# Gated delta attention and squared-ReLU MoE layer on one core: the start of the kernel put in another order, and three weight parts prepared ahead where there were two

## The chip, the cores and the metric

The kernel runs on one core of a Trainium2 chip. The metric is the device time of one execution in microseconds. Besides TensorE (PE, with its weight loads PEld), VectorE (DVE), ScalarE (ACT) and GpSimd (POOL) the core has SyncE (SP), which in this kernel issues every DMA.

## What is computed

For each of 4 batches and 8 heads a 48 by 48 state is carried over 768 tokens: the key is divided by its norm plus 1e-6, the output of a token is its query times the state so far, and then the state takes up beta times the outer product of the key and (value minus what the state holds for that key). The outputs of all heads, 3072 tokens of 384 numbers, go through a layer `relu(x @ w_in)` squared `@ w_out` with 2048 hidden columns. The two weight matrices arrive as 64-bit floats; all else is float32.

## The kernel before

The attention is done in 12 units (`u`), each 128 tokens of two batches with all 8 heads, in two chunks of 64 tokens per head. A unit goes through these stages:

- `load`, `load_q`, `load_beta`, `load_v` (L199 to L230): keys, queries, betas and values, by DMAs of 96 KB (betas 2 KB). A key tile is `kpad`; the second unit's queries use the third `kpad` tile.
- `normalize` (L232): ScalarE squares the keys (L241), VectorE sums them (L242), ScalarE takes the root (L244), VectorE inverts it with one Newton step (L245 to L251) and scales the keys (L253).
- `static` (L263): TensorE transposes keys and queries (L284), ScalarE copies them out (L285), TensorE multiplies keys with keys and keys with queries (L294). For the first two units ScalarE copies the products out (L327, L337) and GpSimd masks the second kind (L340). The triangular blocks go to DRAM and come back in another layout as `lt` (L311, L319).
- `invert` (L353): 31 pairs of VectorE instructions (L380 or L382, and L383), each needing the one before, invert triangular blocks. For the first two units one such chain handles both (`invert(ds_[0])`). The inverse goes to DRAM as `inv` (L389) and comes back as `tt` (L398) and `t1t` (L403); GpSimd clears the second unit's `tt` (L394) once that memory has been read.
- `whole` and `sequential` (L406, L455; together `state_part`, seven pieces): the inverse is completed (L421 to L433), applied (L441, L448), and the state is carried on (L471 to L495).

`moe` (L500) takes a finished unit through the two weight matrices with 3-term products in reduced precision (L540, L527). That needs the weights as a high and a low part. `split_weights` (L135) makes them in 28 parts of 512 or 384 columns, in this order per part: ScalarE takes an absolute value (`least`, L142), GpSimd a maximum (L143), VectorE four bit operations (`words`, L150 to L157), ScalarE copies the high part (L160), TensorE forms the low part with three products (`low`, L166) and ScalarE copies it (L167). A generator does one part per `take`; `low` of a part stands behind `words` of the next. `far` (L173) says how many parts have their `least` written ahead, and `room` (L131) gives the parts scratch tiles alternately from two pools, with two buffers for each name. `fetch(n)` (L122) issues the loads of the next n parts.

Inside `tc.manual_schedule` the order of instructions on PE, SP, DVE and ACT is the order in which the program text emits them. POOL's order is not set by hand. Every engine and SP's queue run their instructions strictly in that order, so an instruction that waits holds back all that stand behind it.

Until L675 the program is written out by hand: loads, the first two units' `normalize` and `static`, the first inverse, the third unit's `normalize` and the first unit's `state_part`, with 19 takes of the split between. This is called the start below. Then a loop (L676) over units 1 to 11 weaves the parts of a unit by fractions of its length (`weave`, L578): the rest of the split (in unit 1 only), the next unit's `static` and `invert`, this unit's `state_part`, loads and `normalize` of the unit after next (`loads`, L599), and the previous unit's `moe`.

Of the kernel before, what the change touches and what calls it, by code (L numbers as in the profile page):

```python
# [20 lines left out]
def kernel(  # L21
# [92 lines left out]
    NW = len(weight_parts)  # L114
# [5 lines left out]
    AHEAD = 20  # L120

    def fetch(n):  # L122
        for _ in range(n):
            x = len(raws)
            if x < NW:
                src = weight_parts[x][2]
                raw = wpool.tile([P, src.shape[1], 2], I32, name=place[x])
                nc.sync.dma_start(out=raw.rearrange("p a b -> p (a b)"), in_=src.bitcast(I32))
                raws.append(raw)
# [5 lines left out]
    def split_weights():  # L135


        def least(x):

            w1 = raws[x][:, :, 1]  # L140
            a, rest = room(x, w1.shape[1])
            nc.scalar.activation(out=a.bitcast(F32), in_=w1.bitcast(F32), func=AF.Abs)  # L142
            nc.gpsimd.tensor_scalar(out=a.bitcast(F32), in0=a.bitcast(F32), scalar1=LEAST, scalar2=None, op0=ALU.max)  # L143
            return x, a, rest

        def words(x, a, rest):
            raw = raws[x]
            w1 = raw[:, :, 1]

            nc.vector.tensor_scalar(out=a, in0=a, scalar1=3, scalar2=0x3FFFFFF8,  # L150
                                    op0=ALU.logical_shift_left, op1=ALU.bitwise_and)

            nc.vector.scalar_tensor_tensor(out=a, in0=w1, scalar=-0x40000000, in1=a,  # L153
                                           op0=ALU.bitwise_and, op1=ALU.bitwise_or)

            nc.vector.tensor_scalar(out=w1, in0=a, scalar1=-0x800000, scalar2=None, op0=ALU.bitwise_and)
            nc.vector.scalar_tensor_tensor(out=rest.bitcast(F32R), in0=raw[:, :, 0].bitcast(U32), scalar=2.0 ** -52,  # L157
                                           in1=w1.bitcast(F32), op0=ALU.mult, op1=ALU.mult)
            hl = wpool.tile([P, 2, raw.shape[1]], F32R, name=place[x])
            nc.scalar.copy(out=hl[:, 0], in_=a.bitcast(F32))  # L160
            return x, a, rest, hl

        def low(x, a, rest, hl, bank):
            ps = bank()[:, :hl.shape[2]]
            for n, (m, y) in enumerate(((ident, a.bitcast(F32)), (minus, hl[:, 0]), (plus, rest.bitcast(F32R)))):
                nc.tensor.matmul(ps, lhsT=m, rhs=y, start=(n == 0), stop=(n == 2))  # L166
            nc.scalar.copy(out=hl[:, 1], in_=ps)  # L167
            halves[weight_parts[x][:2]] = hl[:, 0], hl[:, 1]

        before, ready = None, []  # L170
        for x in range(NW):

            far = 2 if x < AHEAD - 2 else 1  # L173
            while x + len(ready) < min(NW, x + far):
                ready.append(least(x + len(ready)))
            if x == 0:
                yield
            now = words(*ready.pop(0))
            if before:
                low(*before, split_bank)  # L180
            before = now
            if x + 1 + len(ready) < min(NW, x + 1 + far):
                ready.append(least(x + 1 + len(ready)))
            yield
        low(*before, split_bank)
        yield
# [17 lines left out]
    def load(u):  # L204
        t0, b0 = (u // NU) * P, (u % NU) * 2
        d = dict(u=u, t0=t0, b0=b0, y=[None] * NC, marks={})
        d["kp"] = kpad[u % 3]
        load_to(d["kp"], k, d, D)
        return d
# [22 lines left out]
    def normalize(d):  # L232

        n2, s0, s1 = [apool.tile([P, H2], F32, name=f"{n}{d['u'] % 2}", bufs=1) for n in ("n2", "s0", "s1")]
        kn = d["kp"].rearrange("p c h d -> p (c h) d")[:, :, :D]
        for c in range(NC):
            h = slice(c * H, (c + 1) * H)

            sq = (apool.tile([P, H, D], F32, name="r", bufs=2) if d["u"] == 2 else
                  spool.tile([P, PC], F32, name="rest")[:, :H * D].rearrange("p (h e) -> p h e", h=H))  # L240
            nc.scalar.activation(out=sq, in_=kn[:, h], func=AF.Square)  # L241
            nc.vector.tensor_reduce(out=n2[:, h], in_=sq, axis=AX.X, op=ALU.add)  # L242
            yield
        nc.scalar.activation(out=s0, in_=n2, func=AF.Sqrt)  # L244
        nc.vector.tensor_scalar(out=s1, in0=s0, scalar1=1e-30, scalar2=None, op0=ALU.max)  # L245
        nc.vector.reciprocal(out=s1, in_=s1)
        yield
        nc.vector.tensor_tensor(out=s1, in0=s1, in1=n2, op=ALU.mult)
        nc.vector.tensor_tensor(out=s1, in0=s1, in1=s0, op=ALU.add)
        nc.vector.tensor_scalar(out=s1, in0=s1, scalar1=0.5, scalar2=1e-6, op0=ALU.mult, op1=ALU.add)  # L250
        nc.vector.reciprocal(out=s1, in_=s1)  # L251
        yield
        nc.vector.tensor_tensor(out=kn, in0=kn, in1=s1.unsqueeze(2).broadcast_to(list(kn.shape)), op=ALU.mult)  # L253
        yield
# [365 lines left out]
    L1, N1 = (0.22, 0.42), (0.62, 0.92)  # L620
# [7 lines left out]
    engines = {mybir.EngineType.PE, mybir.EngineType.SP, mybir.EngineType.DVE, mybir.EngineType.Activation}  # L628
    with tc.manual_schedule(engines=engines):
        ds_ += [load(0), load(1)]  # L630
        fetch(F0)
        load_beta(ds_[0])
        load_q(ds_[0])
        load_q(ds_[1])
        load_beta(ds_[1])
        fetch(F1)
        take(normalize(ds_[0]))
        take(splits, 1)
        take(normalize(ds_[1]))
        pair = [static(d) for d in ds_[:2]]  # L640
        for d in pair:
            take(d, 2)
# [8 lines left out]
        for d in pair:  # L651
# [5 lines left out]
            take(d, 1)  # L657
            take(splits, 1)
        ds_.append(load(2))
        load_v(ds_[1])  # L660
        load_q(ds_[2])
        load_beta(ds_[2])
        fetch(NW)
        take(invert(ds_[0]))
        third = normalize(ds_[2])
        take(third, 2)
        for _ in range(3):
            take(splits, 1)
            take(third, 1)
# [6 lines left out]
        for u in range(1, units):  # L676
            parts = [(splits, NS, 0, 0.88, "")] if u == 1 else []
            if inverse:
                parts.append((inverse, NI - n_i, 0, I1 - 1, "quiet"))
            getting = loads(u)  # L680
            parts += [(getting, 2, *L1, "quiet"), (getting, 5, *N1, "quiet")]
            if u < units - 1:
                parts.append((static(ds_[u + 1]), 2, *A1))
            parts.append((state_part(ds_[u]), 7, *Q1))
            if before:
                parts += [(before, OVER + 1, 0, E2, ""), (before, 1, 0.2, 0.24, "quiet")]
            before = moe(ds_[u - 1])
            inverse = invert(ds_[u + 1]) if u < units - 1 else None
            if inverse:
                parts.append((inverse, n_i, I0, 1, "quiet"))  # L690
            parts.append((before, n_moe - OVER, M0, M1, ""))
            weave(*parts)
# [32 lines left out]
```

## Time and profile before

| | |
|---|---|
| median of 3 runs | 710.51 us (708.12 to 711.27) |
| the profiled execution | 708.47 us, its span from first to last instruction 706.8 us |
| busy in the span | PE 637.2 us (90%), DVE 427.0 (60%), ACT 332.2 (47%), POOL 73.3 (10%) |
| granted TensorE clock | 0.969 of 2.4 GHz in the mean |

All times of the trace are microseconds from the first instruction. Parts of the weights are numbered from 0 in the order of the split: 0 to 2, 7 to 9 and so on have 512 columns, the others 384. A busy time is the sum over an engine's instructions; an engine that is not busy waits for a semaphore or has its instructions issued late. Busy time on PE is not PE at its peak.

### The profile page before, as it was taken

The page shows a single profiled execution, that of the slowest core. Times are in us where ns is not written, and L with a number is a line of the kernel's source. Part 1 is how long each engine was busy: PE and PEld are TensorE (multiplying, and loading weights), DVE is VectorE, ACT ScalarE, POOL GpSimd, SP SyncE. Part 2 cuts the span into 40 slices and gives each one's busy share as a digit, 9 for nine tenths or more (in the row PEclk, how much of TensorE's full clock was granted, in tenths as well). Part 3 has the DMA queues.
Part 4 walks back from the last instruction along what each step waited for, and adds up shares of the span by engine and source line. Part 5 has one row for each costly group of instructions (what it writes and reads, how often), then busy time and mean ns, then how long its engine had stood idle before and what let it go on. Part 6 is the DMA issues. An engine that isn't in the chain of part 4 may idle for free.

```text
span 706.8 us, 23318 instructions
## 1 busy us (share of the span) xinstructions
PE 637.2 (90%) x10104; PEld 589.9 (83%) x10104; DVE 427.0 (60%) x1165; ACT 332.2 (47%) x632; POOL 73.3 (10%) x86
## 2 busy tenths in 40 slices
PE   1820698798999999999999999999999999999997
PEld 1600267697999999999999999999999999999996
DVE  4789775568468467577576494684675764641111
ACT  3730466454553554544545535535445445355252
POOL 6440342210100100001001001001000010000000
PEclk9965799999999999999999999999999999999999
DMA  7888501400450531522603504406315124030100
GB/s 171 183 221 327 129 3 27 88 2 2 71 105 2 112 65 18 118 43 37 137 5 53 122 3 77 99 4 120 55 21 121 36 38 93 3 61 3 25 1 22
DMA packets 172134, 49.92 MB, mean 71 GB/s; under 512 B 163840, under 2 KB 166912, under 8 KB 172032
## 3 DMA queue, kind: packets, MB, share of 16 engines
q1 hardware_dynamic: 172032, 48.44, 31.7%
q8 instruction: 79, 1.29, 0.8%
q14 instruction: 23, 0.19, 0.1%
HBM read 37.32 MB, written 11.01 MB: 68 GB/s over the span
## 4 chain that ended last, share of the span: by engine, by line
PE 80%; issue 4%; DMA 4%; SPq 3%; DVE 3%; POOL 2%; ACT 2%; POOLq 0%; DVEq 0%
PE h L540 29%; PE o L527 29%; PE g L471 3%; PE g L448 3%; PE g L492 3%; SPq L202 2%; DMA w<-in_moe_w_in_dram 2%; PE x L294 2%; PE x L441 2%; PE x L484 2%; PE x L284 1%; POOL a L143 1%; PE g L284 1%; PE g L294 1%; DMA inv<-tt 1%
## 5 line engine op out<-in xcount | busy, mean ns | idle before, releaser
L527 PE MATMUL o<-w,h_h 128*128 128x384 f32 x768 | 204.2, 347 | 0.0
L540 PE MATMUL h<-x_h,w 128*128 128x256 f32 x1152 | 172.3, 285 | 2.1 <-ACT x_h L509 1.2
L519 DVE TENSOR_TENSOR h_l<-r,h_h 128x512 fp32r<-128x512 f32 x96 | 66.1, 688 | 153.4 <-PE o L527 60.7
L540 PEld LDWEIGHTS h<-x_h,w 128*128 128x128 f32 x1152 | 152.5, 188 | 6.1 <-ACT x_h L509 2.6
L547 ACT ACTIVATE r<-h 128x512 f32<-128x512 f32 x96 | 57.4, 598 | 175.0 <-PE h L540 172.3
L527 PEld LDWEIGHTS o<-w,h_h 128*128 128x128 f32 x768 | 133.9, 189 | 2.5
L527 PE MATMUL o<-w,h_l 128*128 128x384 f32 x384 | 130.2, 339 | 0.0
L382 DVE SCALAR_TENSOR_TENSOR tmp<-lt,bt,z 128x126 f32<-128x126 f32 (+22 forms) x310 | 96.1, 310 | 15.1 <-DMA lt<-blocks 6.7
L540 PE MATMUL h<-x_l,w 128*128 128x256 f32 x576 | 99.0, 280 | 0.0
L383 DVE TENSOR_TENSOR z<-z,tmp 128x126 f32<-128x126 f32 (+22 forms) x310 | 79.2, 255 | 10.6
L540 PEld LDWEIGHTS h<-x_l,w 128*128 128x128 f32 x576 | 81.4, 188 | 0.0
L527 PEld LDWEIGHTS o<-w,h_l 128*128 128x128 f32 x384 | 72.4, 189 | 0.0
L548 ACT ACTIVATE r<-r 128x512 f32<-128x512 f32 x96 | 60.7, 632 | 3.1
L550 ACT CAST h_h<-r 128x512 fp32r<-128x512 f32 x96 | 59.5, 620 | 3.1
L366 POOL MEMSET z<- 128x512 f32 x10 | 5.2, 525 | 397.6 <-DMA inv<-z 397.6
L166 PE MATMUL o<-r,plus 128*128 128x512 f32 (+1 forms) x16 | 9.8, 699 | 30.8 <-DVE r L153 30.8
L242 DVE TENSOR_REDUCE n<-rest 128x8 f32<-128x384 f32 x22 | 12.0, 550 | 38.5 <-ACT rest L241 38.5
L143 POOL TENSOR_SCALAR a<-a 128x384 f32<-128x384 f32 (+1 forms) x18 | 24.2, 1345 | 63.4 <-ACT a L142 48.3
L166 PEld LDWEIGHTS o<-r,plus 128*128 128x128 f32 x16 | 2.9, 219 | 31.8 <-issue 31.6
L433 ACT ACTIVATE tt<-x 32x256 f32<-32x256 f32 x42 | 15.8, 375 | 26.6 <-PE x L429 26.1
L471 PEld LDWEIGHTS g<-state,kq 48*64 48x64 f32 x1408 | 22.5, 134 | 4.3 <-issue 2.5
L509 ACT CAST x_h<-h 128x384 fp32r<-128x384 f32 x24 | 11.4, 481 | 31.1 <-PE h L507 31.1
(141 smaller groups left out, 805.2 us busy)
## 6 DMA issues: line engine op xcount, KB each, us to landing
w<-in_moe_w_in_dram SPq DMA_DIRECT2D x12, 512.0 KB
w<-in_moe_w_out_dram SPq DMA_DIRECT2D x16, 384.0 KB
lt<-blocks SPq DMA_DIRECT2D x22, 256.0 KB
kpad<-in_k_dram SPq DMA_DIRECT2D x48, 96.0 KB
vt<-in_v_dram SPq DMA_DIRECT2D x48, 96.0 KB
out_dram<-a SPq DMA_DIRECT2D x48, 96.0 KB
qpad<-in_q_dram SPq DMA_DIRECT2D x44, 96.0 KB
blocks<-ap SPq DMA_DIRECT2D x48, 64.0 KB
```

What stands on the lines that cost most here:

```text
L143: nc.gpsimd.tensor_scalar(out=a.bitcast(F32), in0=a.bitcast(F32), scalar1=LEAST, scalar2=None, op0=ALU.max)
L294: nc.tensor.matmul(ps[j][b * C:(b + 1) * C, p], lhsT=kq[rows, c, p, b, 0], rhs=kq[rows, c, p, b, first:first + n].rearrange("p x t -> p (x ...
L382: nc.vector.scalar_tensor_tensor(out=tmp, scalar=bt[:, s:s + 1], op0=ALU.mult, op1=ALU.mult, **factors)
L383: nc.vector.tensor_tensor(out=z[:, :nj, s + 1:], in0=z[:, :nj, s + 1:], in1=tmp, op=ALU.subtract)
L448: nc.tensor.matmul(g[rows, c, h], lhsT=tt[rows, c, h], rhs=vt[rows, c, h], start=True, stop=True)
L471: nc.tensor.matmul(dst[b * C:(b + 1) * C, j, p], lhsT=kq[rows, c, p, b, x], rhs=s[rows, b, p], start=(x == 0 and p == 0), stop=False, skip ...
L519: nc.vector.tensor_tensor(out=h_l, in0=r, in1=h_h.bitcast(F32), op=ALU.subtract)
L527: nc.tensor.matmul(o[i], lhsT=a[:, e, i * P:(i + 1) * P], rhs=halves["wo", ft][w], start=(ft == 0 and n == 0), stop=(ft == FT - 1 and n == 2))
L540: nc.tensor.matmul(hp[:, e], lhsT=halves["wi", (kt, ft // EACH)][w][:, f], rhs=x[:, kt], start=(n == 0), stop=(n == 3 * KT - 1))
L547: nc.scalar.activation(out=r, in_=hp, func=AF.Relu)
L548: nc.scalar.activation(out=r, in_=r, func=AF.Square)
L550: nc.scalar.copy(out=h_h, in_=r)
```

## The change

Five edits. In `split_weights` three parts are prepared ahead instead of two until the seventeenth part, then one. In `normalize` a `yield` stands behind the root, so it has six pieces; the two places that count them follow. In the start, the first unit's betas are issued ahead of the first three weight loads, the second unit's `normalize` ahead of the first piece of the split, and the loads of the second unit's values and the third unit's queries and betas behind the inverse's transfers, with the remaining weight loads ahead of the inverse.

```diff
@@ -170,7 +170,7 @@
         before, ready = None, []
         for x in range(NW):
 
-            far = 2 if x < AHEAD - 2 else 1
+            far = 3 if x < AHEAD - 3 else 1
             while x + len(ready) < min(NW, x + far):
                 ready.append(least(x + len(ready)))
             if x == 0:
@@ -179,7 +179,7 @@
             if before:
                 low(*before, split_bank)
             before = now
-            if x + 1 + len(ready) < min(NW, x + 1 + far):
+            while x + 1 + len(ready) < min(NW, x + 1 + (far if x + 1 < AHEAD - 3 else 1)):
                 ready.append(least(x + 1 + len(ready)))
             yield
         low(*before, split_bank)
@@ -242,6 +242,7 @@
             nc.vector.tensor_reduce(out=n2[:, h], in_=sq, axis=AX.X, op=ALU.add)
             yield
         nc.scalar.activation(out=s0, in_=n2, func=AF.Sqrt)
+        yield
         nc.vector.tensor_scalar(out=s1, in0=s0, scalar1=1e-30, scalar2=None, op0=ALU.max)
         nc.vector.reciprocal(out=s1, in_=s1)
         yield
@@ -628,15 +629,15 @@
     engines = {mybir.EngineType.PE, mybir.EngineType.SP, mybir.EngineType.DVE, mybir.EngineType.Activation}
     with tc.manual_schedule(engines=engines):
         ds_ += [load(0), load(1)]
+        load_beta(ds_[0])
         fetch(F0)
-        load_beta(ds_[0])
         load_q(ds_[0])
         load_q(ds_[1])
         load_beta(ds_[1])
         fetch(F1)
         take(normalize(ds_[0]))
+        take(normalize(ds_[1]))
         take(splits, 1)
-        take(normalize(ds_[1]))
         pair = [static(d) for d in ds_[:2]]
         for d in pair:
             take(d, 2)
@@ -657,13 +658,13 @@
             take(d, 1)
             take(splits, 1)
         ds_.append(load(2))
+        fetch(NW)
+        take(invert(ds_[0]))
         load_v(ds_[1])
         load_q(ds_[2])
         load_beta(ds_[2])
-        fetch(NW)
-        take(invert(ds_[0]))
         third = normalize(ds_[2])
-        take(third, 2)
+        take(third, 3)
         for _ in range(3):
             take(splits, 1)
             take(third, 1)
@@ -678,7 +679,7 @@
             if inverse:
                 parts.append((inverse, NI - n_i, 0, I1 - 1, "quiet"))
             getting = loads(u)
-            parts += [(getting, 2, *L1, "quiet"), (getting, 5, *N1, "quiet")]
+            parts += [(getting, 2, *L1, "quiet"), (getting, 6, *N1, "quiet")]
             if u < units - 1:
                 parts.append((static(ds_[u + 1]), 2, *A1))
             parts.append((state_part(ds_[u]), 7, *Q1))
```

## Rows read from the trace of the kernel before

**Rows 1.** Busy time by stretch: length; busy (instructions) of PE, PEld, DVE, ACT, POOL; clock; DMA.
```profile
76.00:77.00 1.00, 0.44 (x2) 0.00 (x0) 0.00 (x0) 0.57 (x2) 1.00 (x2) 0.63 0.67 106
83.00:84.00 1.00, 1.00 (x46) 0.61 (x34) 0.90 (x4) 0.28 (x1) 0.47 (x1) 0.95 0.02 8
86.00:106.00 20.00, 18.19 (x377) 12.57 (x366) 15.62 (x33) 14.27 (x30) 9.21 (x7) 1.00 0.03 6
180.00:660.00 480.00, 480.00 (x8151) 460.43 (x8150) 290.19 (x848) 229.51 (x423) 20.36 (x27) 1.00 0.31 60
```
**Rows 2.** The chain of waits, 40 to 84 us: start, length, what.
```profile
58.62 9.49 DMA w<-in_moe_w_in_dram
68.13 7.65 DMA inv<-tt
```
**Rows 3.** ScalarE in order of time: start, length, instruction, [idle before <-releaser].
```profile
10.62 0.67 ACT L142 ACTIVATE a<-w 128x512 f32<-128x512 f32 x1 [3.28 <-DMA w<-in_moe_w_in_dram]
12.21 0.66 ACT L142 ACTIVATE r<-w 128x512 f32<-128x512 f32 x1 [0.92 <-DMA w<-in_moe_w_in_dram]
...
19.05 0.59 ACT L285 COPY kq<-x 128x512 f32<-128x512 f32 x1 [0.27 <-PE x L284]
...
25.91 0.61 ACT L142 ACTIVATE r<-w 128x384 f32<-128x384 f32 x1
...
35.12 0.56 ACT L142 ACTIVATE a<-w 128x384 f32<-128x384 f32 x1
```
**Rows 4.** VectorE in order of time.
```profile
37.35 0.79 DVE L150 TENSOR_SCALAR a<-a 128x384 int32<-128x384 int32 x1 [1.06 <-POOL a L143]
...
40.32 1.22 DVE L373 TENSOR_TENSOR lt<-lt,bt 128x1024 f32<-128x1024 f32 x1
41.57 0.52 DVE L380 TENSOR_TENSOR h_h<-lt,tt 128x31 f32<-128x31 f32 x1
42.12 0.69 DVE L383 TENSOR_TENSOR tt<-tt,h_h 128x31 f32<-128x31 f32 x1
...
65.56 0.21 DVE L380 TENSOR_TENSOR h_h<-lt,tt 128x31 f32<-128x31 f32 x1
...
68.11 0.42 DVE L150 TENSOR_SCALAR r<-r 128x512 int32<-128x512 int32 x1
...
69.82 0.69 DVE L157 SCALAR_TENSOR_TENSOR h_l<-w 128x512 fp32r<-128x512 uint32 x1
...
77.92 0.72 DVE L150 TENSOR_SCALAR r<-r 128x512 int32<-128x512 int32 x1 [2.15 <-POOL r L143]
```
**Rows 5.** GpSimd in order of time.
```profile
40.36 2.41 POOL L340 TENSOR_SCALAR_AFFINE_SELECT ap<-ap 64x512 f32<-64x512 f32 x2
42.86 1.55 POOL L143 TENSOR_SCALAR a<-a 128x512 f32<-128x512 f32 x1
75.91 0.53 POOL L394 MEMSET tt<- 128x512 f32 x1 [31.50 <-DVE s L251]
```
**Rows 6.** TensorE in order of time.
```profile
82.48 0.94 PE L421 MATMUL x<-tt,ap 32*32 32x32 f32 x64
...
105.70 0.49 PE L507 MATMUL h<-plus,y 128*128 128x128 f32 x3
```
**Rows 7.** SyncE's queue: start of the first issue, length of all, instruction, count.
```profile
7.95 2.78 SPq L224 DMA_DIRECT2D bt<-in_beta_dram  x4
...
28.28 1.52 SPq L319 DMA_DIRECT2D lt<-blocks  x2
...
75.19 1.93 SPq L398 DMA_DIRECT2D tt<-inv  x4
...
84.07 1.78 SPq L403 DMA_DIRECT2D t1t<-inv  x4
```
**Rows 8.** Waits of VectorE from 83.7 to 106 us: total, times, longest.
```profile
DVE a L150 <- POOL a L143: 1.9, 3, 1.4
DVE r L150 <- POOL r L143: 1.0, 2, 0.7
```

## The prediction, made before the changed kernel ran

> **What bounds the kernel now.** I read the busy time by stretch first. From 180 to 660 us TensorE is busy in all 480.00 us at clock 1.00 [rows 1]: the woven units are bound by TensorE, and what this change does to the other engines' order there is worth nothing while TensorE has no gap. All that can move is the start, up to 105.70, where the first `moe` product of the loop runs [rows 6]. If the loop begins x us earlier, the span is x us shorter.
>
> In the start I followed the chain of waits, then each engine in order of time around its links. Four things end last, one after another:
>
> 1. The inverse begins at 40.32 with L373. It is not its data that it waits for but VectorE's order: part 6 of the split stands ahead of it, begins at 37.35 and came late because VectorE was idle 1.06 us for GpSimd's maximum [rows 4]. That maximum waits for ScalarE's absolute value of part 6 at 35.12 [rows 3].
> 2. The inverse itself, 31 dependent pairs on VectorE, until its two transfers are issued (the second at 68.13 [rows 2]).
> 3. From there to L421 at 82.48 [rows 6]. The transfers land 7.65 us after the second issue, behind weight loads (the 9.49 us link ahead of them) [rows 2]. GpSimd clears `tt` only then, at 75.91 [rows 5]; the maximum of part 9 stands behind that on GpSimd, so part 9 begins on VectorE at 77.92 after 2.15 us idle [rows 4], and TensorE's `low` of part 9 stands ahead of L421.
> 4. The first unit's `state_part` with seven parts of the split between, 82.48 to 105.70 [rows 6].
>
> **The change part by part.**
>
> *Betas ahead of the weights, second `normalize` ahead of the split.* Weight parts 0 and 1 are used as they land, at 10.62 and 12.21, 1.59 apart [rows 3]; part 2, now needed at once, would be 1.59 later, 13.80. The four beta issues take 2.78 us of SP's queue [rows 7] and now stand ahead: 16.6. Its absolute value (0.67) ends at 17.3, and the four key copies behind it on ScalarE, 0.59 each at most, at 19.6. Before, the last of them ended at 19.64 [rows 3]. The squares, no longer behind the weights, gain 2 to 3 us for the second unit's keys, but three waits for weights now stand ahead of the copies and take it back. Value 0; as the engines have less to move in front of the weights it may be 1 us better, and if the queries' loads mix into the weights 1 us worse.
>
> *Three parts ahead.* From part 3's absolute value at 25.91 to part 6's at 35.12 [rows 3] three steps took 9.21, 3.07 each. Written one step earlier, the absolute value of part 6 comes 3.07 earlier. VectorE's own work on a part is 2.40 (68.11 to 70.51, 512 columns, [rows 4]), so with the wait for GpSimd gone the three steps can shrink by up to 3 x 0.67 = 2.0. Together 5.0. Bounds: nothing, if ScalarE's waits for landings eat it; at most 6.7, since `lt` must be there: its loads are issued by 29.80 [rows 7] and land between that and 37.45 (with the 7.65 of the loaded queue, [rows 2]), middle 33.6, against 40.32. I take **5.0**. Behind ScalarE's earlier waits for parts 7 to 9 stand query-product copies and high parts that nobody needs before the inverse ends; that cover is some 27 us (40.32 to 68). The scratch tiles, two of each name, alternate between two pools, so part x+3 needs those of part x-1, whose `low` stands just ahead in the text: no new wait.
>
> *GpSimd beside the inverse.* One maximum more (part 9), and later ones, now fall into the inverse. Before, 2.41 + 1.55 = 3.96 us of GpSimd lay beside its first instructions [rows 5], and these were 0.52 and 0.69 where the same shape takes 0.21 at the end [rows 4]: 0.8 us for 3.96. With some 8 us of GpSimd beside it, another 0.8; I take **1.0 lost** (0 to 4).
>
> The Trainium skill (SBUF — State Buffer, Who interferes with whom) speaks against this edit: a VectorE instruction with two SBUF inputs and a GpSimd instruction that reads SBUF exclude one another for the whole of the one that started first. The trace doesn't bear out a whole block: the longest VectorE instruction there is 0.69, not 1.55. By the rule the price is below, as a rival.
>
> *Weights ahead of the inverse, values, queries and betas behind its transfers.* The 15 last weight loads now go out 13 issues earlier, some 9 us (three groups of four at 2.78 [rows 7] and one copy), so they no longer stand ahead of `inv`, or only by their last two. So the maximum of part 9 (now also written ahead of the clearing of `tt`) is there before the inverse ends, and GpSimd's wait for `inv` holds only part 10. What is late next is VectorE: parts 7 and 8 at 2.40 and six small `normalize` instructions at about 0.21 (the smallest VectorE length in [rows 4]; an estimate) put part 9 6.1 us after part 7. L421 came 4.56 after part 9 began (82.48 - 77.92, at half clock), so 10.7 after part 7, where it was 82.48 - 68.11 = 14.4. Gain **3.7**. Bounds: 2.0, if parts cost the 2.97 that part 6 took beside GpSimd (37.35 to 40.32) and `normalize` more; 5.5, if `low` runs at full clock. The transfers are no bound: the inverse ends near 63.3; if two weight loads are left, `inv` lands by 66.5, and with the 7.3 us that before lie between 75.2 (the issue of `tt` [rows 7]) and L421, `tt` is there by 73.8, and L421 wants it at 74.8.
>
> The 13 moved issues stand behind the last `t1t` loads, which wait for VectorE's transpose of the first unit (84.07 to 85.85 before [rows 7], about 77 after). They are out by 86 and landed by 90. The queries are needed first, by the third unit's transposes just behind 105.70, after the change about 96.5. Value 0, cover 6 us; every us beyond it costs one.
>
> *Split beside `state_part`.* VectorE waits 1.9 + 1.0 = 2.9 us there for GpSimd [rows 8], which a part more ahead takes away. But TensorE is busy 18.19 of 20 us [rows 1], so not all of it comes back: between 0 and 2.9, I take **1.5**.
>
> *Six pieces of `normalize`, one part ahead from part 17 on.* The root is issued a piece before VectorE reads it. In the loop TensorE has no gap to win. From part 19 on one part less is ready than before, in a loop whose first unit has TensorE gaps: 0, from 1 better to 1 worse.
>
> Sum: 5.0 - 1.0 + 3.7 + 1.5 = 9.2 us. Against the profiled execution, 708.47 (span 706.8 and 1.67 around it), that is 699.3. This execution was 2.04 below the median of three, 710.51; against that the same 9.2 gives **701.3**, which I predict.
>
> **The rivals.**
>
> *Only the second half comes* (0.14). ScalarE's in-order waits for parts 2 and 7 to 9 keep the inverse's begin where it is. For: parts 0 and 1 both waited for their landing [rows 3]. Against: the maximum of part 6 is written ahead of those waits. Gain 3.7 + 1.5 = 5.2: 705.3.
>
> *GpSimd blocks VectorE in the inverse* (0.07). As a mechanism of this kernel: each of the 8 us of GpSimd beside the inverse stops VectorE wholly, so it gains 8.0 - 0.8 = 7.2 us of length in place of 1.0, and 9.2 becomes 3.0: 707.5. For: 0.52 and 0.69 for 0.21. Against: 0.8 us lost beside 3.96, a fifth. It is the rule named above.
>
> *More than forecast* (0.09). All waits for GpSimd go and `low` runs at full clock: 6.7 - 0.5 + 5.0 + 2.9 = 14.1: 696.4.
>
> *No gain* (0.07). The loop's first unit, not the start, ends last: with one part less ready its 11 parts lose some 0.8 us each, near 9.2 in all: 710.5. Against: VectorE had room there.
>
> *Slower: the clock* (0.07). TensorE idles through the inverse and its clock falls to half; after a gap at 76 to 77 it fell again (0.63) and was back only in 83 to 84 (0.95) [rows 1], just as `state_part` began. If the earlier and more broken burst of `low` leaves it at half through `state_part`, the 18.19 busy us of that stretch cost as much again: 9.2 - 18.2 = 9.0 lost, 719.5. It decides from the point where more than half of the stretch runs at half clock. Against: it came back here within the first us of `state_part`, and that work is as dense after the change.
>
> **How the numbers follow.** Forecast 0.56, with its own range 698 to 704; the others as given. To hold 8 in 10 the range leaves out the slower case, most of no gain, and a little of each end: 695 to 708. A measurement of this kernel can't tell less than about 0.5% (3.6 us) from no change. Faster takes the forecast, half a share of the blocking case, the half gain and the larger gain: 0.83. Same: no gain and the rest of the blocking case, 0.10. Slower: 0.07.
>
> **What would show it.** L373 near 35; the inverse some 28 us long; `inv` landing within 4 us of its issue; part 9 starting without a wait for GpSimd; L421 near 75; the first L507 near 96.5; 180 to 650 as before. I am wrong if L373 stays near 40, if SP's late loads end the wait of the third unit's transposes, or if the loop's first unit shows new TensorE gaps.

## The result, and the profile after

The changed kernel takes 702.82 us in the median of 4 runs (700.77 to 705.31), the kernel before 710.25 us beside it: a ratio of 0.9893, 95% interval 0.9859 to 0.9927. It is faster by 7.4 us; 701.3 us was predicted, with a range of 695 to 708. The profile is of the fastest of the four: 700.77 us, with a span of 699.1.

In the new code all lines from L245 on stand one further down, so L374 is the L373 of before, L422 the L421 and L508 the L507. The busy time by stretch of the changed kernel comes first, with the columns of [rows 1]; the stretch 78 to 100 is the `state_part` of the first unit, as 86 to 106 was before.

```profile
70.00:71.00 1.00, 1.00 (x3) 0.69 (x3) 0.86 (x3) 0.41 (x1) 0.66 (x2) 0.54 0.74 115
76.00:77.00 1.00, 1.00 (x67) 0.68 (x65) 0.86 (x3) 0.50 (x2) 0.42 (x1) 1.00 0.23 35
78.00:100.00 22.00, 19.39 (x420) 13.74 (x421) 19.11 (x38) 15.14 (x32) 8.30 (x6) 1.00 0.25 45
180.00:650.00 470.00, 470.00 (x8028) 450.74 (x8027) 287.45 (x842) 223.56 (x414) 15.63 (x24) 1.00 0.31 60
```

The woven units are bound by TensorE as before (470.00 of 470.00 us). In the start VectorE is now almost as full as TensorE (19.11 against 19.39 of 22), and TensorE's clock is whole from 71 on, ahead of L422 at 76.28; before, it was still at half when L421 began at 82.48 and was back in 83 to 84 [rows 1]. Next the chain of waits: start, length, what.

```profile
65.77 3.05 DMA inv<-tt
```

The inverse has landed at 68.82, 3.1 us after it is done on VectorE; before, it had landed at 75.78, 8.5 us after (68.13 and 7.65 [rows 2]). Now VectorE of the changed kernel in order of time: start, length, instruction, and in brackets the idle time before it and who ended it.

```profile
35.38 0.36 DVE L150 TENSOR_SCALAR a<-a 128x384 int32<-128x384 int32 x1 [1.06 <-POOL a L143]
...
37.38 1.22 DVE L374 TENSOR_TENSOR lt<-lt,bt 128x1024 f32<-128x1024 f32 x1
...
64.45 1.23 DVE L386 TENSOR_TENSOR tt<-tt,bt 128x1024 f32<-128x1024 f32 x1
...
66.52 0.42 DVE L150 TENSOR_SCALAR r<-r 128x512 int32<-128x512 int32 x1
...
68.84 0.17 DVE L246 TENSOR_SCALAR s<-s 128x16 f32<-128x16 f32 x1
...
72.38 0.36 DVE L150 TENSOR_SCALAR r<-r 128x512 int32<-128x512 int32 x1
```

Part 6 of the split (35.38) still waits 1.06 us for GpSimd, as before [rows 4], and the inverse begins at 37.38. Part 9 (72.38) waits for nobody. ScalarE shows what holds part 6:

```profile
28.65 0.59 ACT L142 ACTIVATE r<-w 128x384 f32<-128x384 f32 x1
...
33.11 0.55 ACT L142 ACTIVATE a<-w 128x384 f32<-128x384 f32 x1 [2.43 <-DMA w<-in_moe_w_out_dram]
```

Its absolute value at 33.11 waits 2.43 us for the landing of its own weights. That is a new bound; in the kernel before this instruction ran at 35.12 without a wait [rows 3]. ScalarE was free for it at 30.68. GpSimd and TensorE:

```profile
69.63 0.53 POOL L395 MEMSET tt<- 128x512 f32 x1 [20.80 <-DVE a L150]
```
```profile
76.28 0.75 PE L422 MATMUL x<-tt,ap 32*32 32x32 f32 x64
...
99.38 0.49 PE L508 MATMUL h<-plus,y 128*128 128x128 f32 x3
...
101.22 0.66 PE L285 MATMUL x<-plus,qpad 128*128 128x128 f32 x4 [0.92 <-ACT w L167]
```

The loop's first `moe` product stands at 99.38, 6.3 us ahead of its 105.70 [rows 6]. The third unit's queries, whose loads were moved, are there in time: their transposes at 101.22 wait for a copy of ScalarE, not for a DMA. From one milestone to the next:

| stretch | before | after | change | predicted |
|---|---|---|---|---|
| until the inverse begins (L374) | 40.32 | 37.38 | -2.9 | -5.0 |
| the inverse, to the end of L386 | 27.0 | 28.3 | +1.3 | +1.0 |
| from there to L422 | 15.2 | 10.6 | -4.6 | -3.7 |
| L422 to L508 | 23.2 | 23.1 | -0.1 | -1.5 |
| first unit of the loop | 69.0 | 67.7 | -1.3 | 0 |
| all the rest | | | -0.1 | 0 |

The sum is -7.7, the difference of the spans (706.8 and 699.1). The 1.3 us of the loop's first unit (from its first L508 to the next unit's, 99.38 to 167.06) are a stretch of half clock: the mean clock from 134 to 150 us was 0.89 before, and over the whole unit it is 1.00 after.

```profile
134.00:150.00 16.00, 13.00 (x240) 11.27 (x238) 11.33 (x32) 9.61 (x19) 3.37 (x3) 0.89 0.01 3
```

(this row is of the kernel before). Two runs of the changed kernel took 700.8 and 701.3 us at a mean clock of 0.978, two took 704.4 and 705.3 at 0.968 and 0.966. That fits such stretches in some executions of one and the same kernel, though it isn't shown for these, which have no trace. I don't count those 1.3 us as the change's.

### The profile page after: what moved, and what is told of

It reads as the page before. It is cut to its first block, busy times and chain, and to the rows that moved or that the text cites. A ratio compares the mean times of both kernels' runs of the same rounds, so it can differ in the third digit from the quotient of the medians.

```text
span 699.1 us, 23322 instructions
## 1 busy us (share of the span) xinstructions
PE 635.6 (91%) x10104; PEld 590.5 (84%) x10104; DVE 429.0 (61%) x1165; ACT 331.7 (47%) x632; POOL 69.6 (10%) x86
## 4 chain that ended last, share of the span: by engine, by line
PE 80%; DVE 9%; SPq 3%; ACT 3%; issue 2%; DMA 1%; POOL 1%; DVEq 0%; POOLq 0%
PE h L541 29%; PE o L528 29%; PE g L472 3%; PE g L493 3%; PE g L449 3%; DVE h_h L381 2%; SPq L202 2%; DVE tt L384 2%; PE x L442 2%; PE x L485 2%; PE x L295 1%; PE g L295 1%; PE g L285 1%; PE x L285 1%; DVE a L153 1%
## 5 line engine op out<-in xcount | busy, mean ns | idle before, releaser
L384 DVE TENSOR_TENSOR z<-z,tmp 128x126 f32<-128x126 f32 (+22 forms) x310 | 79.2, 255 | 10.7
L472 PE MATMUL g<-state,kq 48*64 48x48 f32 x1408 | 25.3, 220 | 0.0
```

Source lines behind the costliest of these rows:

```text
L384: nc.vector.tensor_tensor(out=z[:, :nj, s + 1:], in0=z[:, :nj, s + 1:], in1=tmp, op=ALU.subtract)
L472: nc.tensor.matmul(dst[b * C:(b + 1) * C, j, p], lhsT=kq[rows, c, p, b, x], rhs=s[rows, b, p], start=(x == 0 and p == 0), stop=False, skip ...
```

## The experiments

Unless it says otherwise, each is the changed kernel with the edit shown, and "later" is against the milestones of the changed kernel.

One profile of each was taken, and that limits what small differences mean. In six of the runs (the loads back, the root back, the two made lighter, and both with more GpSimd) all that leads up to the inverse's begin is the changed kernel's own. There the inverse begins at 38.01 to 38.41, not at 37.38, as in these two:

```profile
38.04 1.22 DVE L374 TENSOR_TENSOR lt<-lt,bt 128x1024 f32<-128x1024 f32 x1
```
```profile
38.41 1.22 DVE L374 TENSOR_TENSOR lt<-lt,bt 128x1024 f32<-128x1024 f32 x1
```

(the first with six maxima more, the second with seventeen fills more). Part 6's weights were there for ScalarE at 34.10 to 34.50 in the six, at 33.11 in the changed kernel's profile. So the begin, and every milestone behind it, differs by up to 1.0 us between executions of the same code, and the changed kernel's profile is the earliest of the seven. The lengths of the stretches behind the begin are steadier; a table behind the runs has them.

**Two parts ahead again.**

```diff
-            far = 3 if x < AHEAD - 3 else 1
+            far = 2 if x < AHEAD - 2 else 1
-            while x + 1 + len(ready) < min(NW, x + 1 + (far if x + 1 < AHEAD - 3 else 1)):
+            while x + 1 + len(ready) < min(NW, x + 1 + far):
```

> The changed kernel with two parts prepared ahead again, all else as changed. Theory A (the third part ahead is what lets the inverse begin earlier, and what frees part 9 from the clearing of tt): the inverse begins near 40 instead of 37.4, its chain is some 1 us shorter (less GpSimd work beside it), part 9 begins on VectorE only after the inverse's transfers have landed, L422 (the first product with tt) near 80 to 81 instead of 76.3, total 3 to 5 us above the changed kernel, 706 to 708. Rival B (looking further ahead is worth something only beside state_part): the inverse still begins near 37.4 and L422 stays near 76.3, but the stretch from L422 to the first L508 grows from 23.1 by 2 to 3 us. If A holds and the stretch stays 23.1, the VectorE waits for GpSimd that stood in it were covered.

Measured: 703.58 us, ratio to before 0.9901 (0.9869 to 0.9933). The inverse began 1.65 us later (39.03), was 0.9 shorter, L422 came 0.9 later and L508 1.45 later (100.83). Against the six other begins of the same code it is 0.6 to 1.0 later. So the third part ahead is worth between 0.3 and 1.5 us at the loop's begin, half or less of the 3 to 5 that the first theory gave it. The maximum of part 9 now stands behind the clearing of `tt`, but with `inv` landing early, it holds nobody up.

**The betas behind the first weights again.**

```diff
-        load_beta(ds_[0])
         fetch(F0)
+        load_beta(ds_[0])
```

> The changed kernel with the first unit's betas behind the first three weight loads again. Theory A (in the changed kernel the start is now held by landings: part 6 is waited for by ScalarE until 33.1, and the betas ahead of the weights moved all landings back): the absolute value of part 2 comes at 13.5 to 14.5 instead of 16.2, part 6 lands near 31.5, the inverse begins near 35.5, total 1 to 2.5 us below the changed kernel, 700 to 702. Rival B (the second unit's keys are what ends last, and SP's queue is late for another reason): the inverse begins at 37.0 to 37.8 as with the change, total within 0.5 us of it.

Measured: 702.28 us, ratio 0.9870 (0.9838 to 0.9902). L374 at 36.49 and L508 at 98.46, both 0.9 us earlier; against the six other begins L374 is 1.5 to 1.9 earlier. ScalarE:

```profile
32.00 0.56 ACT L142 ACTIVATE a<-w 128x384 f32<-128x384 f32 x1 [0.16 <-DMA w<-in_moe_w_out_dram]
```

Part 6 hardly waits for its weights, and VectorE goes from part 5 to part 6 without a wait. So the betas ahead cost 0.9 to 1.9 us at the loop's begin, near the first theory's 1 to 2.5; the time is too close to the changed kernel's to tell.

**The loads ahead of the inverse again.**

```diff
-        fetch(NW)
-        take(invert(ds_[0]))
         load_v(ds_[1])
         load_q(ds_[2])
         load_beta(ds_[2])
+        fetch(NW)
+        take(invert(ds_[0]))
```

> The changed kernel with the second unit's values and the third unit's queries and betas issued ahead of the remaining weights and the inverse again. Theory A (the moved loads shorten the transfers' wait, and that is a part of what L422 gained): the inverse's transfers land 75 to 76 instead of 69.5, tt near 78.5, L422 near 79.5 to 80, total 3 to 4 us above the changed kernel, 706 to 707. Rival B (VectorE's order of parts 7 to 9 ends last, the transfers are hidden): L422 stays at 76 to 76.5 and the total within 0.7 us of the changed kernel.

Measured: 710.18 us, ratio 0.9997 (0.9972 to 1.0023): the whole gain is gone, twice what the first theory had for it. First VectorE, then TensorE:

```profile
78.02 0.65 DVE L150 TENSOR_SCALAR a<-a 128x384 int32<-128x384 int32 x1 [1.86 <-POOL a L143]
...
82.97 0.45 DVE L415 STREAM_TRANSPOSE t<-t1t 128x256 f32<-128x256 f32 x1 [2.47 <-DMA t1t<-inv]
```
```profile
78.58 0.22 PE L422 MATMUL x<-tt,ap 32*32 32x32 f32 x2 [1.86 <-DMA tt<-inv]
```

The inverse lands as late as before (`tt` is issued at 75.62). Part 9, whose maximum now stands ahead of the clearing, begins at 72.94 without a wait; it is L422 itself that waits 1.86 us for `tt` to land, then the clearing at 76.33 holds the maximum of part 10, and the transpose of `t1t` waits 2.47 us for its landing. L508 comes 5.0 us later, 0.7 of it by the begin. The loop's first unit takes 72.2 us in place of 67.7, with 10.2 us at half clock in it; in the run with two parts ahead it takes 71.1, so this is not put down to the loads.

**The second `normalize` behind the first piece of the split again.**

```diff
         take(normalize(ds_[0]))
-        take(normalize(ds_[1]))
         take(splits, 1)
+        take(normalize(ds_[1]))
```

> The changed kernel with the second unit's normalize behind the first piece of the split again, so that its squares wait for three weight landings on ScalarE. Theory A (with three parts ahead this order is dear, the new order of normalize is needed by it): the second unit's keys are scaled near 20.5 instead of 14.8, the copies of the keys end 4 us later, the inverse begins near 41, total 3 to 4 us above the changed kernel, 706 to 707. Rival B (the copies wait for the weights anyway, so the squares' place is worth nothing, as the prediction had it: value 0): the inverse begins within 0.7 us of 37.4.

Measured: 706.25 us, ratio 0.9934 (0.9914 to 0.9955). ScalarE:

```profile
16.42 0.66 ACT L142 ACTIVATE a<-w 128x512 f32<-128x512 f32 x1 [1.05 <-DMA w<-in_moe_w_in_dram]
16.99 0.92 ACT L241 ACTIVATE rest<-kpad 128x384 f32<-128x384 f32 x2
```

The second unit's squares stand behind three waits for weights, until 16.99; its keys are scaled at 21.19 instead of 14.82, the inverse begins 3.5 us later (2.4 to 2.8 against the six) and L508 comes 3.6 later, as the first theory had it. With three parts ahead this order is worth the most of all that moves the inverse's begin.

**The loads' move alone, in the kernel before.**

```diff
+        fetch(NW)
+        take(invert(ds_[0]))
         load_v(ds_[1])
         load_q(ds_[2])
         load_beta(ds_[2])
-        fetch(NW)
-        take(invert(ds_[0]))
```

> The kernel before with one edit alone: the second unit's values and the third unit's queries and betas issued behind the inverse's transfers, the remaining weights ahead of it. Theory A (this edit takes the weights out of the way of the inverse's transfers, so all that stood on their landing moves, but the inverse itself begins no earlier): the inverse begins at 40 to 40.5 and ends near 67.3, its transfers land near 71 instead of 75.8, GpSimd clears tt near 71, L421 near 78 to 78.5, the first L507 near 101.5 to 102, total 3.5 to 4.5 us below before, 706 to 707. Rival B (taking this edit out of the changed kernel cost the whole gain, so it is the whole gain): total 702.5 to 704, the other edits then being worth nothing by themselves or together with it.

Measured: 707.84 us, ratio 0.9972 (0.9957 to 0.9988); L507 at 105.41, 0.3 us ahead of the kernel before. Both theories fail: the median is 2.1 us under the 709.91 of the kernel before beside it, where the first had 3.5 to 4.5. VectorE:

```profile
73.94 0.58 DVE L245 TENSOR_SCALAR s<-s 128x16 f32<-128x16 f32 x1 [1.75 <-ACT s L244]
...
77.78 0.36 DVE L150 TENSOR_SCALAR r<-r 128x512 int32<-128x512 int32 x1
```

The transfers are 3.0 us earlier (`tt` issued at 72.15) and part 9 no longer waits for GpSimd, but it begins at 77.78 all the same: VectorE waits 1.75 us for the third unit's root, and the inverse began 1.3 us later than before (41.59), in code that the edit doesn't touch. From the inverse's end to L421 it takes 13.2 us in place of 15.2, and that is what the move alone is worth. Taking the one wait away brought the other to light.

**The root in one piece with its readers again.**

```diff
         nc.scalar.activation(out=s0, in_=n2, func=AF.Sqrt)
-        yield
-        take(third, 3)
+        take(third, 2)
-            parts += [(getting, 2, *L1, "quiet"), (getting, 6, *N1, "quiet")]
+            parts += [(getting, 2, *L1, "quiet"), (getting, 5, *N1, "quiet")]
```

> The changed kernel with one of its small edits undone: the third unit's square root stands again in one piece with the maximum and the reciprocal that use it, behind part 10's ScalarE work, so that 2 pieces instead of 3 run behind the inverse, and the loop's pieces are 5 again. The prediction gave this edit 0. Theory A: it is a part of the gain, since VectorE then waits for the root again as it did in the kernel before (1.75 us at the line of the maximum) while parts 9 and 10 stand behind it: L422 1 to 2 us later than the 76.28 of the changed kernel, and L508 with it, time 1 to 2 us over the changed kernel's 702.8. Theory B: the wait is covered by TensorE's own work of parts 10 to 13, so L422 and L508 move by less than 0.5 us and the time stays within 1 us. Theory C: the six pieces in the loop are what helps: L508 is unmoved, and the loop units are each longer, by over 0.1 us.

Measured: 704.18 us, ratio 0.9920 (0.9893 to 0.9947). L422 at 79.60, 3.3 us later, L508 2.9 later; 0.6 of it is the inverse's later begin, which this edit doesn't touch. From the inverse's end to L422 it takes 13.4 us in place of 10.6. First VectorE, then TensorE of this run:

```profile
71.08 0.47 DVE L245 TENSOR_SCALAR s<-s 128x16 f32<-128x16 f32 x1 [1.63 <-ACT s L244]
```
```profile
73.35 2.04 PE L166 MATMUL o<-a,plus 128*128 128x512 f32 x2 [1.97 <-DVE a L153]
...
76.41 2.04 PE L166 MATMUL o<-r,plus 128*128 128x512 f32 x2
```

On ScalarE the root stands behind the copy of part 7's high part, which needs VectorE's work on part 7; so VectorE waits 1.63 us for an answer that in the changed kernel is there before it is asked for (L246 at 68.84, no wait). TensorE's products come later with it and still run at half clock: two of part 9 take 2.04 us, where in the changed kernel they take 1.10:

```profile
73.61 1.10 PE L166 MATMUL o<-r,plus 128*128 128x512 f32 x2 [0.51 <-DVE r L153]
```

Theory A has the mechanism. That L422 moves by more than its 1 to 2 us goes with the half clock; how much of it is the clock's was not tried.

**TensorE's work in `state_part` made lighter** (the first of the three products of `low` left out for parts 10 to 16).

```diff
-                nc.tensor.matmul(ps, lhsT=m, rhs=y, start=(n == 0), stop=(n == 2))
+                if not (light and n == 0):
+                    nc.tensor.matmul(ps, lhsT=m, rhs=y, start=(n == int(light)), stop=(n == 2))
```

> The changed kernel with the first of the three products that form the low part left out for parts 10 to 16 (their low parts are then not the weights'): TensorE does 0.55 to 0.85 us less for each of the seven parts that stand beside the first unit's state_part. Theory A (TensorE's own in-order work bounds the stretch from L422 to the first L508, which is why taking away VectorE's waits bought nothing): the stretch falls from 23.1 to 18.5 to 20.5. Rival B (VectorE's four operations on a part bound it): it stays within 0.7 us of 23.1.

Measured: 708.48 us, a single run. L422 to L508 took 27.1 us instead of 23.1. The same 27 us of both kernels, this one first (the changed kernel's hold 4.6 us of the loop):

```profile
77.00:104.00 27.00, 24.16 (x467) 18.99 (x467) 19.51 (x39) 15.33 (x33) 9.44 (x7) 0.56 0.20 37
```
```profile
77.00:104.00 27.00, 22.42 (x440) 15.68 (x438) 20.80 (x41) 18.86 (x41) 10.21 (x8) 1.00 0.21 37
```

With less to do TensorE ran at a mean clock of 0.56 (half from 79.7 to 103.6) instead of 1.00, and was busy longer. Why the clock fell in this one execution is not shown. Neither theory is tested by it, but it shows the price of the clock there: 4 us and more.

**VectorE's work made lighter** (two of the four bit operations left out for parts 11 to 17).

```diff
-            nc.vector.tensor_scalar(out=w1, in0=a, scalar1=-0x800000, scalar2=None, op0=ALU.bitwise_and)
+            if not light:
+                nc.vector.tensor_scalar(out=w1, in0=a, scalar1=-0x800000, scalar2=None, op0=ALU.bitwise_and)
```

(and the same at L150)

> The changed kernel with two of the four VectorE operations left out for parts 11 to 17 (these weights are then not right): VectorE does about 0.8 us less for each of the parts beside the first unit's state_part, 5 to 6 us in all. Theory A (TensorE's in-order work bounds the stretch from L422 to the first L508): it stays within 0.7 us of 23.1. Rival B (VectorE bounds it): it falls to 18 to 20.

Measured: 702.47 us, a single run. L422 to L508 took 21.05 us, 2.05 less, for some 5.5 us of VectorE work left out. VectorE's waits from 77 to 98 us (total, times, longest; the update of the state stands three lines further down here):

```profile
DVE state L491 <- PE h L488: 4.4, 1, 4.4
```

It gives 4.4 us of it back at once, waiting for TensorE to update the state; in the changed kernel that wait is 1.0. Both theories miss: the stretch is bound by VectorE and TensorE in turn.

**Six more GpSimd maxima beside the inverse, then seventeen fills.** The two kernels differ in one line:

```diff
+        for _ in range(6):
+            nc.gpsimd.tensor_scalar(out=scr, in0=scr, scalar1=LEAST, scalar2=None, op0=ALU.max)
...
+        for _ in range(17):
+            nc.gpsimd.memset(scr, 0.0)
```

> The changed kernel with six more GpSimd maxima over 128x512 on scratch memory beside the inverse, where GpSimd is idle (from about 50 us on, some 9 us of GpSimd work that reads and writes SBUF; nothing needs the result). Theory A (a VectorE instruction beside such work takes some 0.3 to 0.45 us longer once per GpSimd instruction, as the 2.4 us lost beside 7.3 us of it in the changed kernel say): the inverse's chain from L374 to the end of L386 grows from 28.3 by 2.5 to 3.5. Rival B (no more than the two engines' shared access, a small tax): by less than 1. Rival C (the two exclude one another for a whole GpSimd instruction, the Trainium skill's rule in SBUF - State Buffer, Who interferes with whom): by 8 to 9.

> The changed kernel with seventeen more fills of 128x512 by GpSimd on a scratch tile beside the inverse, some 7 to 10 us of work that writes and reads nothing, in the place where an earlier run had six maxima that read two operands and lengthened the inverse by 1.6 us. Theory A: it is GpSimd's reading that lengthens VectorE's instructions, so the inverse stays within 0.5 us of 28.3 us. Theory B: any GpSimd instruction does it, at about 0.3 us each, so seventeen cost 3 to 5 us, and the inverse takes 31 to 33 us. The time, one look, goes with it: 702 to 705 by A, 705 to 709 by B.

Measured: 704.63 and 701.82 us, a single run each. GpSimd of the first and of the second:

```profile
49.79 9.89 POOL L665 TENSOR_SCALAR x_h<-x_h 128x512 f32<-128x512 f32 x6 [0.83 <-ACT x_h L663]
```
```profile
50.72 9.85 POOL L665 MEMSET x_h<- 128x512 f32 x17 [1.68 <-ACT x_h L663]
```

The same 9.9 us of GpSimd lengthen the inverse from 28.30 to 29.93 us where it reads, and leave it at 28.32 where it only writes. VectorE beside the maxima:

```profile
51.30 0.42 DVE L381 TENSOR_TENSOR h_h<-lt,tt 128x252 f32<-128x252 f32 x1
51.76 0.71 DVE L384 TENSOR_TENSOR tt<-tt,h_h 128x252 f32<-128x252 f32 x1
52.50 0.42 DVE L381 TENSOR_TENSOR h_h<-lt,tt 128x255 f32<-128x255 f32 x1
52.96 0.42 DVE L384 TENSOR_TENSOR tt<-tt,h_h 128x255 f32<-128x255 f32 x1
53.42 0.71 DVE L381 TENSOR_TENSOR h_h<-lt,tt 128x256 f32<-128x256 f32 x1
```

Each maximum of 1.65 us (9.89 / 6) lengthens one VectorE instruction, by 0.29 us, and the two or three behind it run free. The fills fit theory A of their run. For the maxima the 1.6 us lie between the two nearer theories, and the 8 to 9 us of a whole block are out. (The Trainium skill, SBUF — State Buffer, Who interferes with whom, says of two-input VectorE instructions that they contend with a GpSimd instruction that reads, not with one that only writes; these two runs agree. That the one that came later is fully blocked for a whole instruction, they do not show: 0.29 of 1.65 us.)

**The weights asked for earlier: a version meant to be faster.**

```diff
-        load_beta(ds_[0])
         fetch(F0)
         load_q(ds_[0])
+        fetch(F1 + 1)
         load_q(ds_[1])
+        load_beta(ds_[0])
         load_beta(ds_[1])
-        fetch(F1)
...
-        fetch(1)
```

(the last line is the load of part 6 behind the blocks)

> A version that is to beat the changed kernel: the first three parts of the weights and the next two are asked for directly behind the first k loads, between the q loads, and the betas behind all of them, and the early loading of the last of them behind the blocks goes. In the changed kernel the landing of part 6's weights at 33.1 sets when the inverse begins (ScalarE waits 2.43 us for it). Theory A: that landing is the bound, so the inverse's multiply (L374 there) comes 2 to 3 us earlier, at 34.5 to 35.5, L508 at 96.5 to 97.5, and the time 2 to 3 us under the changed kernel's 702.8. Theory B: the q loads and so the second half of the first two units' products come late instead, and the blocks' transfers or the last selects end as late as before: L374 within 0.7 us of 37.4, and the time within 1 us. Theory C: the inverse begins earlier but TensorE's clock falls to half in the first loop unit, and the unit's 67.7 us become 70 or more, so the time is 702 to 705.

Measured: 700.65 us (697.45 to 701.51), ratio to before 0.9864 (0.9839 to 0.9889). VectorE:

```profile
35.06 1.22 DVE L374 TENSOR_TENSOR lt<-lt,bt 128x1024 f32<-128x1024 f32 x1 [0.58 <-DMA lt<-blocks]
```

Theory A: the inverse begins 2.3 us earlier than in the changed kernel's profile (3.0 to 3.4 against the six) and now waits, for 0.58 us, for its own data, so more cannot be had from the weights. L508 stands at 96.87, 2.5 us earlier. The profiled execution (701.34 us) gives that back, as theory C had it: the loop's first unit takes 70.7 us, with the clock at half for 6.8:

```profile
156.00:164.00 8.00, 8.00 (x103) 7.43 (x103) 4.26 (x18) 2.42 (x5) 0.00 (x0) 0.57 0.01 2
```

It beats the kernel before. Its median is 2.2 us under the changed kernel's, but the two intervals overlap, so that it beats that one too is likely and not shown.

**The stretches side by side** (us; L374, L422 and L508 are the L373, L421 and L507 of before):

| run | L374 begins | the inverse | its end to L422 | L422 to L508 |
|---|---|---|---|---|
| kernel before | 40.32 | 27.0 | 15.2 | 23.2 |
| changed kernel | 37.38 | 28.3 | 10.6 | 23.1 |
| seventeen fills | 38.41 | 28.3 | 10.6 | 23.1 |
| two parts ahead | 39.03 | 27.4 | 10.7 | 23.7 |
| betas back | 36.49 | 28.2 | 10.6 | 23.1 |
| loads back | 38.11 | 28.2 | 12.2 | 25.8 |
| `normalize` back | 40.85 | 28.3 | 10.6 | 23.2 |
| root back | 38.01 | 28.2 | 13.4 | 22.7 |
| loads alone, in the kernel before | 41.59 | 27.4 | 13.2 | 23.2 |
| weights earlier | 35.06 | 28.0 | 10.6 | 23.1 |

## Why the prediction was right, and where it was off

*The bound was where it was said to be.* All but the 1.3 us of clock came from the start: L508 moved by 6.3 us, and the woven units stayed at TensorE's pace. Of the seven signs named, the woven units' pace, the inverse's length (28.30), its landing (3.05 us after issue) and part 9 without a wait came as said; L374 (37.4, not 35) and the two milestones behind it (76.3 and 99.4, not 75 and 96.5) came late.

*Three parts ahead, 5.0: mis-sized, 2.9 in the profile and 1.9 to 2.3 in the six others.* Two things went into the 5.0, a step of 3.07 us won and 2.0 us of shorter steps. On ScalarE they nearly came: it was free for part 6 at 30.68, 4.4 us ahead of 35.12. What took 2.43 us of it back is the case that I had kept for the lower bound, the wait for a landing, at part 6's own weights (33.11). I had bounded the begin by the landing of `lt` and not worked out the landing of the weights, whose last load is issued only behind the blocks, at 29.08. The wait for GpSimd behind it stayed at 1.06. The last 1.0 us came from a term that I did not have: GpSimd is idle beside part 6 on VectorE, and its four operations take 2.00 us (35.38 to 37.38), not 2.97 [rows 4]. My 2.40 for VectorE's own work was that of 512 columns; parts 3 to 6 have 384. The third part itself is worth 0.6 to 1.65 us of the begin (two parts ahead again: 39.03). Asking for the weights earlier took the begin to 35.06, the figure I had forecast, and there `lt` ends the wait, as my bound had it.

*The order of `normalize` and betas, 0: right as a net, of terms that are not small.* I set the squares' gain against three waits for weights ahead of the key copies, and had the last copy end at 19.6, as before [rows 3]. It ends at 18.82:

```profile
18.22 0.60 ACT L286 COPY kq<-x 128x512 f32<-128x512 f32 x1
```

But the order is not worth nothing: with three parts ahead and the squares behind the weights again, that copy ended at 23.86 (23.27 + 0.59) and the inverse began 3.5 us later. It pays for what the third part puts in the way. The betas cost 0.9 to 1.9.

*GpSimd beside the inverse, -1.0: -1.3.* The mechanism is the one read from [rows 4] and [rows 5], though a third lengthened instruction stands there behind the two that I counted (0.51, where the same shape takes 0.22 at the end), which makes 1.1 us of my 0.8:

```profile
43.10 0.51 DVE L383 TENSOR_TENSOR tt<-tt,h_h 128x60 f32<-128x60 f32 x1
```

But its measure is not GpSimd's time. It is one VectorE instruction lengthened for each GpSimd instruction that reads. Beside the changed kernel's inverse stand three maxima and four masking instructions, and seven VectorE instructions are lengthened, as 0.77 and 0.73 here:

```profile
41.45 0.77 DVE L381 TENSOR_TENSOR h_h<-lt,tt 128x156 f32<-128x156 f32 x1
42.26 0.32 DVE L384 TENSOR_TENSOR tt<-tt,h_h 128x156 f32<-128x156 f32 x1
42.61 0.34 DVE L381 TENSOR_TENSOR h_h<-lt,tt 128x175 f32<-128x175 f32 x1
42.99 0.73 DVE L384 TENSOR_TENSOR tt<-tt,h_h 128x175 f32<-128x175 f32 x1
```

The rival in which GpSimd blocks VectorE for its whole time is refuted by the six maxima.

*The loads moved, 3.7: 4.6 in that stretch, and more than half of it not by the loads alone.* I let VectorE run parts 7 to 9 one behind the other, 6.1 us from the begin of part 7 to that of part 9. It was 5.86 (66.52 to 72.38), and L422 came 3.90 behind part 9, at full clock, where I had 4.56 at half. But I gave all of it to the loads, and VectorE can run so only with the root a piece earlier, which I had put at 0. The loads' move alone shortens the stretch by 2.0 us, and without the root's edit it is 2.8 longer. I had looked only at who waits for GpSimd there, and not at VectorE's 1.75 us wait for ScalarE in the kernel before, which stood ahead of the one I saw:

```profile
72.26 0.17 DVE L245 TENSOR_SCALAR s<-s 128x16 f32<-128x16 f32 x1 [1.75 <-ACT s L244]
```

With the loads ahead again, part 9 is not held either, as its maximum stands ahead of the clearing; what ends the wait then is the landing of `tt`, which I had called no bound.

Undone one at a time, the four edits (third part, loads, `normalize`, root) cost 1.45, 5.0, 3.6 and 2.9 us at L508, 13 in all for a gain of 6.3. Up to 1 us of each is the begin that differs by execution; the table of stretches shows the rest. Between the inverse and L422 the loads (1.6) and the root (2.8) nearly add up to the 4.6. The surplus lies elsewhere: with the loads back, L422 to L508 takes 2.7 us more, though the kernel before was not slow there, and the order of `normalize` is worth its 2.4 to 3.5 with the third part ahead, which puts one more wait for weights in its way; by itself it was not tried. What an edit is worth depends on which others stand.

*`state_part`, 1.5: nothing (0.1).* The waits for GpSimd there went, as the waits of VectorE from 76 to 100 us show beside [rows 8]:

```profile
DVE state L488 <- PE h L485: 1.0, 1, 1.0
DVE r L475 <- PE g L472: 0.2, 1, 0.2
```

But the stretch did not shorten. I took half of the waits back because TensorE was 91% busy; VectorE's 19.11 of 22 us now fill the rest, and taking 5.5 us of them away shortens it by 2.05.

*The moved issues, 0 with 6 us of cover:* right (101.22 waits for no DMA). *The slower rival, the clock:* it did not come in the changed kernel. Its price is real, as the run with less `low` shows: the stretch of 23.1 us then took 27.1, with a part of TensorE's work gone. The 18 us that I had put on it no run tests.

In the sum, errors of +2.1, +0.3, -0.9, +1.4 and -1.3 (the last is the clock in the loop's first unit, which varies by execution) left the forecast 1.5 us low, and the likeliest case held. That it came so near is in part luck: two terms too large were made up for by an edit priced at nothing and by the clock.

## What to carry to other kernels

Before a move is priced at nothing, list every wait in the stretch that it shortens, on every engine, and the landing of every load that the earlier instruction needs: the wait next in line sets what the move is worth. What an edit is worth depends on which others stand, so each is tried with the others in place and by itself, and read stretch by stretch. Where the same code begins a stretch at times 1 us apart, a milestone that moved by less says nothing. And a change on an engine that is idle part of the time should be read with TensorE's granted clock beside it, since it can cost more than the work that was moved.

## What the runs showed of the hardware that was not expected

- TensorE with less work was slower in the one run made: with one product in three of `low` left out its clock stood at half for 23.9 us, and the stretch grew from 23.1 to 27.1 us.
- GpSimd instructions that read lengthen one two-input VectorE instruction each (0.29 us for maxima of 1.65 us); 9.85 us of fills lengthen none. VectorE's bit operations are lengthened too: the same 128x384 one takes 0.79 us beside GpSimd (37.35 in [rows 4]) and 0.36 with GpSimd idle (35.38 after).
- Stretches at half clock inside the loop's first unit differ from execution to execution: none in the changed kernel's profile, 3.4 us in the kernel before, 10.2 with the loads back. The changed kernel's two longer runs have the lower mean clocks, but with two parts ahead 705.75 us went with 0.973 and 702.99 with 0.970, so they don't explain the whole spread. What starts them stays open.
